# Splitting weight rounding in two steps, moving denominators and T3, and summing attention weights on VectorE and GpSimd instead of by DMA

## The chip, the cores and the metric

The kernel runs on one core of one Trainium2 chip. The metric is the device time of one execution in microseconds, as the median of several runs. Beside it there is a profile of one execution. The engines are called as the profile calls them: PE (TensorE), DVE (VectorE), ACT (ScalarE), POOL (GpSimd) and SP (SyncE, which issues transfers).

## What is computed

The program is an attention block with routing, followed by a bilinear feed-forward block. Each query and each key is assigned to the nearest of 16 centroids, and a query sees only the keys of its own cluster.

```python
batch, n_heads, seq, head_dim = (4, 8, 768, 64)      # 16 clusters
q_assign = np.argmax(np.einsum('bhsd,hcd->bhsc', q_n, c_n), axis=-1)
k_assign = np.argmax(np.einsum('bhsd,hcd->bhsc', k_n, c_n), axis=-1)
mask = q_assign[:, :, :, None] == k_assign[:, :, None, :]
scores = np.where(mask, scale * np.matmul(q, k.transpose(0, 1, 3, 2)), -1e9)
attn = np.exp(scores - np.max(scores, axis=-1, keepdims=True))
attn = attn / (np.sum(attn, axis=-1, keepdims=True) + 1e-09)
x = np.matmul(attn, v)          # heads side by side: 3072 tokens of 512
a = x @ w_a                     # 512 x 1536
b = x @ w_b                     # 512 x 1536
out = (a * b) @ w_out           # 1536 x 512
```

The three weight matrices are float64, and have to be rounded to float32 on the chip.

## The kernel before

Two heads are handled together as a pair. There are 16 pairs, 4 to a batch, and the tokens of a pair are handled in two halves of 384. The main loop goes by groups, six to a pair and so three to a half. In each group TensorE computes two tiles of scores, ScalarE takes their exponential (`pt`, 128 keys by 2 heads by 384 queries), and the tiles of the group before are multiplied with the values. The rest of a group is filled with pieces of the feed-forward block, which belong to the batch before.

```python
for g in range(NG + 3):
    ...
    if 0 < g < NG:
        score(now)                     # TensorE, then the exponential on ScalarE
    check_inverses()
    if 0 < g <= NG:
        for u in before:
            add_up(u)                  # sums of the exponentials over the keys
    if 1 < g <= NG:
        weigh(before)                  # TensorE: times the values
    late = int(g > EARLY)
    if g % 3 == late and 0 < g - late:
        denominators(*divmod(g // 3 - 1, 2))
    ...
    parts = due.get(g, [])             # weight parts to be rounded in this group
    def round_next():
        if parts or not ffn:
            see_w()
        if parts:
            round_w(parts.pop(0))
    round_next()
    ...
    while len(ffn) > least and credit > 0:
        cost, piece = ffn.popleft()
        credit -= cost
        piece()                        # a product of the feed-forward block
        if todo:
            todo.popleft()()           # a step of assignment or normalization
        round_next()
```

The sum over the keys is needed for the denominator. The six tiles (j = 0 to 5) of a half are added into one tile `acc`, whose partitions are then summed by a product with ones. For the pairs of the first batch (p < HP) VectorE adds. For the later ones VectorE adds the first two tiles, and the other four come by accumulating DMAs that GpSimd issues:

```python
def add_up(u):
    p, hf, j = where(u)
    ...
    if j == 1:
        nc.vector.tensor_tensor(out=acc, in0=probs[u - 1], in1=probs[u],
                                op=ALU.add)                        # L595
    else:
        nc.gpsimd.dma_start(out=acc, in_=probs[u], accum_op=ALU.add)  # L598

def denominators(p, hf):
    ps = apart()                       # a bank of the scores' pool
    ... matmul(ones, acc) per head     # L629
    nc.scalar.activation(out=den, in_=ps[:, 0:HB], func=AF.Copy, ...)  # L634
```

The weights are rounded in 36 parts of 128x512. Four instructions on VectorE build the upper part and the remainder, and GpSimd adds both. There is one buffer `rest` and two buffers `raw`. The check of sizes (`see_w`) on ScalarE frees `raw` for the next part.

```python
def round_w(i):
    nc.vector.tensor_scalar(out=wi, in0=hi, ...)                    # L280
    nc.vector.scalar_tensor_tensor(out=wi, in0=hi, in1=wi, ...)     # L283
    rest = wtp.tile([P, WN], FP32, name="rest")
    nc.vector.tensor_scalar(out=rest.bitcast(INT32), in0=wi, ...)   # L287
    nc.vector.scalar_tensor_tensor(out=rest, in0=lo, in1=rest, ...) # L290
    nc.gpsimd.tensor_tensor(out=w, in0=w, in1=rest, op=ALU.add)     # L292
    unseen.append(...)

due = {3 * i + 1: [i] for i in range(8)}
for i in range(8, len(w_parts)):
    due.setdefault(26 + int((i - 8) / 1.5), []).append(i)
```

The feed-forward block multiplies 2 by 2 blocks with seven products instead of eight. For this it needs combinations: T1 to T4 of x (`combine_x`, L779, 128x768, VectorE) and S1 to S4 of the weights (L798, 128x256, VectorE). The products come in the order p1, p2, p6, p5, p7, p3, p4, over three banks. p6 reads T2, p5 T1, p7 T3 and p4 T4. ScalarE copies a first result from its bank (L830), VectorE adds further ones (L834), and GpSimd multiplies a by b (L840). GpSimd also multiplies x by the inverse denominators (L661). In the first batch T2 is made when the last x of the batch is normalized, and T3 with the second product:

```python
        else:                                    # ffn_ready, first batch
            h = h_first
            combine_x(0, "T2")
            ffn.extend(ups_first + plain_ups(0, h, range(NF - 4, NF)))
...
            elif n == 0:                         # ffn_ups, first batch
                ps[1] = both(ps[1], lambda: combine_x(b, "T3"))
                ps[3] = both(lambda: combine_x(b, "T4"), ps[3])
```

A downward stage of each batch (`ffn_downs`) multiplies with w_out in the same manner; its combinations are L929 (weights) and L938 (h).

Of the kernel before, what the change touches and what calls it, by code (L numbers as in the profile page):

```python
# [8 lines left out]
FP32 = mybir.dt.float32  # L9
BF16 = mybir.dt.bfloat16  # L10
INT32 = mybir.dt.int32
UINT32 = mybir.dt.uint32
INT64 = mybir.dt.int64
AF = mybir.ActivationFunctionType
ALU = mybir.AluOpType
# [127 lines left out]
def short_path(nc, tc, ctx, c, cn, centroids_in, casts, n_far, q, k, v,  # L143
# [121 lines left out]
    def load_w(i):  # L265
        if i >= len(w_parts):
            return
        raw = rawp.tile([P, WN], INT64, name="raw")
        nc.sync.dma_start(out=raw, in_=w_parts[i][1])
        raws[i] = raw  # L270

    def round_w(i):
        w = w_parts[i][0]
        wi = w.bitcast(INT32)
        raw = raws.pop(i)
        halves = lambda dt: raw.bitcast(dt).rearrange("p (n two) -> p n two", two=2)
        lo, hi = halves(UINT32)[:, :, 0], halves(INT32)[:, :, 1]


        nc.vector.tensor_scalar(out=wi, in0=hi, scalar1=3, scalar2=0x3FFFFFF8,  # L280
                                op0=ALU.logical_shift_left,
                                op1=ALU.bitwise_and)
        nc.vector.scalar_tensor_tensor(out=wi, in0=hi, scalar=SIGN_TOP, in1=wi,  # L283
                                       op0=ALU.bitwise_and, op1=ALU.bitwise_or)

        rest = wtp.tile([P, WN], FP32, name="rest")
        nc.vector.tensor_scalar(out=rest.bitcast(INT32), in0=wi,  # L287
                                scalar1=SIGN_EXP, scalar2=None,
                                op0=ALU.bitwise_and)
        nc.vector.scalar_tensor_tensor(out=rest, in0=lo, scalar=2.0 ** -52,  # L290
                                       in1=rest, op0=ALU.mult, op1=ALU.mult)
        nc.gpsimd.tensor_tensor(out=w, in0=w, in1=rest, op=ALU.add)  # L292
        unseen.append((i, halves(FP32)[:, :, 1]))

    unseen = []

    def see_w():

        while unseen:
            i, upper = unseen.pop()
            size = spare()[0].bitcast(BF16)[:, 3 * WN:4 * WN]
            nc.scalar.activation(out=size, in_=upper, func=AF.Abs)
            n = 4 * NPAIR + i
            nc.scalar.activation(out=size, in_=size, func=AF.Relu, scale=-STEEP,
                                 bias=edge[:, 0:1], accum_out=stat[:, n:n + 1])
            load_w(i + 2)

    NSTAT = 4 * NPAIR + len(w_parts)  # L310
    edge = zero.tile([P, 1], FP32, name="edge")
# [271 lines left out]
    def add_up(u):  # L583
        p, hf, j = where(u)
        if j == 0 or j == NJ - 1 and p < HP:
            return
        if j == 1:
            accs[p, hf] = accp.tile([P, 2, HB], FP32, name="acc")
        acc = accs[p, hf]
        if p < HP:  # L590
            nc.vector.tensor_tensor(out=acc, in0=probs[u - 1] if j == 1 else acc,  # L591
                                    in1=probs[u], op=ALU.add)
            return
        if j == 1:
            nc.vector.tensor_tensor(out=acc, in0=probs[u - 1], in1=probs[u],  # L595
                                    op=ALU.add)
        else:
            nc.gpsimd.dma_start(out=acc, in_=probs[u], accum_op=ALU.add)  # L598

    def weigh(us):  # L600
        for u in us:
# [141 lines left out]
    def spare():  # L743
        if "spare" not in W:
            W["spare"] = [combp.tile([P, n], FP32, name=name) for name, n in (
                ("pair", 2 * WN), ("comb", 2 * P))]
        return W["spare"]
# [25 lines left out]
    def combine_x(b, name):  # L773
        x = xTs[b]
        l, r = {"T3": (x[:, 2:4, HB:S], x[:, 0:2, HB:S]),
                "T1": (x[:, 0:2, HB:S], x[:, 0:2, 0:HB]),
                "T2": (x[:, 2:4, HB:S], W["T1"]),
                "T4": (x[:, 2:4, 0:HB], W["T2"])}[name]
        nc.vector.tensor_tensor(out=W[name], in0=l, in1=r, op=ALU.subtract)  # L779

    def ffn_ups(b, h):
# [109 lines left out]
        for n, (combinations, ps) in enumerate(parts):  # L891
            if n == 0 and b:
                ps[0] = both(*combinations, ps[0])
                ps[2] = both(lambda: combine_x(b, "T4"), ps[2])
            elif n == 0:
                ps[1] = both(ps[1], lambda: combine_x(b, "T3"))
                ps[3] = both(lambda: combine_x(b, "T4"), ps[3])
            if n + 1 < len(parts):
                for i, step in enumerate(parts[n + 1][0], 4):
                    ps[i] = both(ps[i], step)  # L900
            pieces += [(2 * HB, f) for f in ps]
# [10 lines left out]
    def ffn_downs(b, h):  # L912
# [96 lines left out]

        def before():  # L1010
            see_w()
            assert not raws
            down_room()
            tiles[0][0]()
            combine_w("T1", "12", "11")
            combine_w("T2", "22", "T1")
# [13 lines left out]
    def both(*fs):  # L1030
        return lambda: [f() for f in fs]
# [5 lines left out]
    def early_steps():  # L1037
        combinations = []

        def begin():  # L1040
            early_room(h_first)
            steps, pieces = ffn_ups(0, h_first)
            ups_first.extend(pieces)
            combinations.extend(steps)

        last = HP * GPP
        return {last - 8: lambda: (begin(), combine_x(0, "T1")),
                last: lambda: [f() for f in combinations[0:2]],
                last + 1: lambda: combinations[2]()}

    def ffn_ready(p, hf):

        b, hp = divmod(p, HP)
        if hp < HP - 1 or hf == 0:
            return
        if b > 0:
            h = []

            ffn.insert(len(ffn) - FREE_ROOM, (0, lambda: (
                up_room(b), combine_x(b, "T3"), combine_x(b, "T1"))))  # L1060
            ffn.insert(len(ffn) - 1, (0, lambda: combine_x(b, "T2")))
            ffn.extend(ffn_ups(b, h)[1])
        else:
            h = h_first
            combine_x(0, "T2")
            ffn.extend(ups_first + plain_ups(0, h, range(NF - 4, NF)))
        ffn.extend(ffn_downs(b, lambda: h))

# [14 lines left out]

    due = {3 * i + 1: [i] for i in range(8)}
    for i in range(8, len(w_parts)):
        due.setdefault(26 + int((i - 8) / 1.5), []).append(i)
    early = early_steps()

    for _ in range(12):
        nc.tensor.matmul(out=idle[0:D, 0:D], lhsT=ones, rhs=ones, start=True,  # L1090
# [31 lines left out]
    for g in range(NG + 3):  # L1122
        p, l = divmod(g, GPP)
        if l == 0:
            ready = prep_steps(p + 1)
        now = (2 * g, 2 * g + 1)
        before = (2 * g - 2, 2 * g - 1)
        if g == 1:
            weigh(before)
        if 0 < g < NG:  # L1130
            score(now)
# [3 lines that stand above are left out]
                add_up(u)  # L1135
        if 1 < g <= NG:
            weigh(before)
        late = int(g > EARLY)
        if g % 3 == late and 0 < g - late:
            denominators(*divmod(g // 3 - 1, 2))  # L1140
        if g < NG:
            ready[l]()
        parts = due.get(g, [])
        if g in early:
            todo.append(early[g])

        def round_next():
            if parts or not ffn:
                see_w()
            if parts:  # L1150
                i = parts.pop(0)
                round_w(i)

        round_next()
        if g <= EARLY:
            first, second = 4, 1
        else:
            first, second = 5, 3 if g < NG else 2
        ph = {first: (p, 0), second: (p - 1, 1)}.get(l)
        halved = ph in den_of  # L1160
        if halved:
            todo.extend(normalize(*ph))
        if ffn:
            credit += PER_GROUP[(g > 2 * BG + 3) + (g > 3 * BG + 3)]
            least = FREE_ROOM if halved and ph[1] and (ph[0] + 1) % HP == 0 else 0
# [3 lines that stand above are left out]
                piece()  # L1169
                if todo:  # L1170
                    todo.popleft()()
                round_next()
        else:
            credit = 0
        round_next()
        while todo:
            todo.popleft()()
        if halved:
            ffn_ready(*ph)
        if l == 0 and p + 1 < NPAIR:  # L1180
            if p and not by_blocks(p + 1):
                prep_transpose(p + 1, 2)
            load(p + 2)
        if l == 4 and p + 1 < NPAIR and not by_blocks(p + 1):
            prep_onehot(p + 1, 0)
# [265 lines left out]
```

## Time and profile before

| | |
|---|---|
| time, median of 3 runs | 1055.83 us (1055.52 to 1056.8) |
| span of the profiled execution | 1052.8 us |
| mean granted clock of TensorE | 0.995 |
| exponential, L572 (ScalarE) | 192 x 808 ns |
| accumulating DMA, L598: issue on GpSimd, landing | 96 x 862 ns, 4.0 us |
| first add of a later half, L595 (VectorE) | 24 x 1042 ns |
| multiplication a by b, L840 (GpSimd) | 66 x 1110 ns |
| rounding, L290 (VectorE), L292 (GpSimd) | 36 x 692 ns, 36 x 1402 to 1434 ns |

The profile gives for each engine the time in which it was busy, and for a group of equal instructions their number and mean duration. Idle time before an instruction is put down to what ended it. "A <- B: x, n, y" means that A waited for B for x us in total, n times, at most y us. A row of busy times by stretch has, after the bounds and the length, the busy time of PE, of PE's weight loads, of DVE, ACT and POOL, each with the number of instructions, then the granted clock of TensorE, the busy share of the DMA engines and GB/s. A row of the timeline has the start, the duration, the engine, the line and the operation, and in brackets the idle time before it.

### The profile page before, as it was taken

How to read it: one execution, taken by the hardware profiler on the slowest of the kernel's cores; microseconds unless marked ns; L12 is line 12 of the kernel's file. 1: busy time of each engine (PE TensorE's matmuls, PEld its weight loads, DVE VectorE, ACT ScalarE, POOL GpSimd, SP SyncE). 2: the span in 40 equal slices, each digit the busy share in tenths (PEclk: the TensorE clock that was granted, in tenths of full speed). 3: DMA queues.
4: the chain of work that ended last, by engine and by line, in shares of the span. 5: the costliest groups of instructions: out<-in, count | busy, mean ns of one | idle time of the engine just before them, and what ended most of it. 6: DMA issues, size and time to landing. Idle time of an engine off the chain costs nothing.

```text
span 1052.8 us, 17688 instructions
## 1 busy us (share of the span) xinstructions
PE 1023.8 (97%) x7094; PEld 499.5 (47%) x7094; DVE 579.2 (55%) x1098; ACT 336.5 (32%) x674; POOL 254.1 (24%) x251
## 2 busy tenths in 40 slices
PE   8999989989999999999999999999999999999997
PEld 5443333334445554444444655444444566444564
DVE  6668777786658345443545535444443635444552
ACT  5666544444542213333233121233232201111100
POOL 1112234354332112222324211232222110212100
PEclk9999989999999999999999999999999999999999
DMA  7334546857574463626243372533322320000000
GB/s 181 87 83 88 102 90 147 167 129 154 140 156 86 94 112 65 109 46 106 54 81 65 78 134 54 91 61 66 60 45 50 76 56 21 1 1 1 6 31 29
DMA packets 134346, 84.24 MB, mean 80 GB/s; under 512 B 108144, under 2 KB 117360, under 8 KB 134256
## 3 DMA queue, kind: packets, MB, share of 16 engines
q0 software_dynamic: 13824, 37.75, 19.8%
q1 hardware_dynamic: 120016, 44.85, 19.0%
q8 instruction: 58, 0.95, 0.4%
q10 hardware_dynamic: 416, 0.43, 0.1%
q14 instruction: 32, 0.26, 0.1%
HBM read 37.78 MB, written 6.29 MB: 42 GB/s over the span
## 4 chain that ended last, share of the span: by engine, by line
PE 80%; DMA 6%; DVE 6%; issue 4%; POOL 2%; ACT 2%; DVEq 0%; POOLq 0%; SPq 0%; ACTq 0%
PE m L692 54%; PE s L563 12%; PE O L606 10%; DMA acc<-pt 5%; PE s L629 1%; PE m L629 1%; PE s L378 1%; DVE acc L591 1%; ACT pt L572 1%; PE m L378 1%; POOL xT L661 0%; DVE acc L595 0%; POOL acc L598 0%; POOL h L840 0%; PE m L362 0%
## 5 line engine op out<-in xcount | busy, mean ns | idle before, releaser
L572 ACT ACTIVATE pt<-s 128x768 f32<-128x768 f32 x192 | 146.2, 808 | 191.1 <-PE s L563 142.6
L598 POOL DMA_DIRECT2D acc<-pt x96 | 82.8, 862 | 261.1 <-DMA acc<-pt 161.5
L606 PE MATMUL O<-pt,v 128*64 128x384 f32 x768 | 145.0, 499 | 0.0
L563 PE MATMUL s<-qkT 64*128 64x384 f32 x768 | 140.3, 484 | 0.0
L840 POOL TENSOR_TENSOR h<-h,ha 128x384 f32<-128x384 f32 x66 | 72.8, 1110 | 214.6 <-DVE ha L834 213.7
L834 DVE TENSOR_TENSOR ha<-ha,m 128x384 f32<-128x384 f32 x88 | 48.1, 549 | 126.7 <-PE m L692 100.9
L830 ACT COPY h<-m 128x384 f32<-128x384 f32 x88 | 42.2, 480 | 213.3 <-PE m L692 209.9
L834 DVE TENSOR_TENSOR h<-h,m 128x384 f32<-128x384 f32 x88 | 48.2, 547 | 100.9 <-PE m L692 73.5
L606 PEld LDWEIGHTS O<-pt,v 128*64 128x64 f32 x768 | 46.6, 136 | 85.8 <-issue 77.9
L692 PE MATMUL m<-wo_sb,h 128*64 128x256 f32 x768 | 86.7, 379 | 0.0
L692 PE MATMUL m<-xT,wa_sb 128*64 128x384 f32 x480 | 83.7, 487 | 2.7 <-DVE ha L834 2.5
L563 PEld LDWEIGHTS s<-qkT 64*128 64x128 f32 x768 | 71.0, 188 | 31.8 <-issue 0.9
L692 PE MATMUL m<-xT,wb_sb 128*64 128x384 f32 x480 | 83.1, 486 | 0.4 <-DVE h L834 0.4
L692 PE MATMUL m<-raw 128*64 128x384 f32 x432 | 78.9, 486 | 0.0
L692 PEld LDWEIGHTS m<-wo_sb,h 128*64 128x64 f32 x768 | 56.1, 137 | 29.1 <-issue 3.7
L661 POOL TENSOR_TENSOR xT<-xT,acc 128x384 f32<-128x384 f32 x32 | 35.2, 1099 | 133.4 <-DVE acc L656 84.1
L692 PE MATMUL m<-xT,h 128*64 128x256 f32 x576 | 64.6, 379 | 0.0
L692 PE MATMUL m<-xT,pair 128*64 128x384 f32 x352 | 64.5, 487 | 0.0
L830 ACT COPY ha<-m 128x384 f32<-128x384 f32 x66 | 31.6, 478 | 98.8 <-PE m L692 93.2
L692 PEld LDWEIGHTS m<-xT,wa_sb 128*64 128x64 f32 x480 | 34.9, 137 | 46.1 <-issue 33.2
L692 PEld LDWEIGHTS m<-xT,wb_sb 128*64 128x64 f32 x480 | 34.6, 137 | 43.5 <-issue 37.0
L692 PEld LDWEIGHTS m<-xT,h 128*64 128x64 f32 x576 | 42.1, 137 | 21.4 <-issue 1.6
(180 smaller groups left out, 1323.6 us busy)
## 6 DMA issues: line engine op xcount, KB each, us to landing
acc<-pt POOLq DMA_DIRECT2D x96, 384.0 KB, 4.0
raw<-in_moe_w_a_dram SPq DMA_DIRECT2D x12, 512.0 KB, 4.2
raw<-in_moe_w_b_dram SPq DMA_DIRECT2D x12, 512.0 KB, 3.7
raw<-in_moe_w_out_dram SPq DMA_DIRECT2D x12, 512.0 KB, 3.9
qk<-in_q_dram SPq DMA_DIRECT2D x48, 96.0 KB, 3.3
qk<-in_k_dram SPq DMA_DIRECT2D x48, 96.0 KB, 3.7
v<-in_v_dram SPq DMA_DIRECT2D x24, 192.0 KB, 3.9
out_dram<-rest SPq DMA_DIRECT2D x24, 128.0 KB, 1.7
```

What stands on the lines that cost most here:

```text
L378: nc.tensor.matmul(out=ps[32 * kq:32 * kq + 32, 0:HB], lhsT=cTb[:, hp, :], rhs=qkTs[p][:, kq * HB:(kq + 1) * HB], start=True, stop=True)
L563: nc.tensor.matmul(out=s[:, a, 0:HB], lhsT=Ts[p][r, S + j * P:S + (j + 1) * P], rhs=Ts[p][r, hf * HB:(hf + 1) * HB], start=start, stop=not ...
L572: nc.scalar.activation(out=pt, in_=s[:, :, 0:HB], func=AF.Exp, scale=SCALE)
L591: nc.vector.tensor_tensor(out=acc, in0=probs[u - 1] if j == 1 else acc, in1=probs[u], op=ALU.add)
L598: nc.gpsimd.dma_start(out=acc, in_=probs[u], accum_op=ALU.add)
L606: nc.tensor.matmul(out=O_of[0][a * D:(a + 1) * D, 0:HB], lhsT=vs[p][:, a, j, :], rhs=probs[u][:, a, :], start=(j == 0), stop=(j == NJ - 1))
L629: nc.tensor.matmul(out=ps[a * D:(a + 1) * D, 0:HB], lhsT=ones, rhs=t[:, a, :], start=(n == 0), stop=(n == len(terms) - 1))
L661: nc.gpsimd.tensor_tensor(out=x, in0=x, in1=den, op=ALU.mult)
L692: nc.tensor.matmul(out=ps[half], lhsT=lhsT[:, half], rhs=rhs, **kw)
L830: nc.scalar.copy(out=box[name], in_=box["X"][:, 0:HB])
L834: nc.vector.tensor_tensor(out=box[name], in0=box[name], in1=box[bank][:, 0:HB], op=ALU.add)
L840: nc.gpsimd.tensor_tensor(out=to, in0=to, in1=box[name], op=ALU.mult)
```

## The change

Four things change. A part of the weights is rounded in two steps, `first` and `second`, with products between them, and the steps run after products and no longer ahead of a group's first one; parts fall due at 1.6 instead of 1.5 a group. The denominators are computed behind the second product of a group. T3 is made right behind T2 in the first batch. The sums of the later batches are made by VectorE and GpSimd, by heads: VectorE takes the first head up to j = 3, GpSimd the second head, and both heads for j = 4 and 5. The purpose is that products find their operands and banks ready, and that the sums need no transfers.

```diff
     def round_w(i):
...
+        def first():
+            see_w()
+            hi = halves(INT32)[:, :, 1]
+            nc.vector.tensor_scalar(out=wi, in0=hi, ...)
+            nc.vector.scalar_tensor_tensor(out=wi, in0=hi, ...)
+
+        def second():
+            rest = wtp.tile([P, WN], FP32, name="rest")
+            nc.vector.tensor_scalar(out=rest.bitcast(INT32), in0=wi, ...)
+            nc.vector.scalar_tensor_tensor(out=rest, ...)
+            nc.gpsimd.tensor_tensor(out=w, in0=w, in1=rest, op=ALU.add)
+            unseen.extend(see_steps(i))
+
+        return [first, second]
...
-        if j == 1:
-            nc.vector.tensor_tensor(out=acc, in0=probs[u - 1], in1=probs[u],
-                                    op=ALU.add)
-        else:
-            nc.gpsimd.dma_start(out=acc, in_=probs[u], accum_op=ALU.add)
+        for a in range(2):
+
+            eng = nc.gpsimd if a == 1 or j > 3 else nc.vector
+            eng.tensor_tensor(
+                out=acc[:, a, :],
+                in0=probs[u - 1][:, a, :] if j == 1 else acc[:, a, :],
+                in1=probs[u][:, a, :], op=ALU.add)
...
             elif n == 0:
-                ps[1] = both(ps[1], lambda: combine_x(b, "T3"))
                 ps[3] = both(lambda: combine_x(b, "T4"), ps[3])
...
             combine_x(0, "T2")
+            combine_x(0, "T3")
             ffn.extend(ups_first + plain_ups(0, h, range(NF - 4, NF)))
...
-        due.setdefault(26 + int((i - 8) / 1.5), []).append(i)
+        due.setdefault(26 + int((i - 8) / 1.6), []).append(i)
...
-        if g % 3 == late and 0 < g - late:
-            denominators(*divmod(g // 3 - 1, 2))
+        halves = [divmod(g // 3 - 1, 2)] if g % 3 == late and 0 < g - late else []
+
+        def sums_across():
+            while halves:
+                denominators(*halves.pop())
+
+        if not ffn:
+            sums_across()
+        pieces = 0
...
-        round_next()
+        if not ffn:
+            see_w(1)
+            round_next()
...
                 piece()
                 if todo:
                     todo.popleft()()
-                round_next()
+                for _ in range(cost // HB // 2):
+                    round_next()
+                pieces += 1
+                if pieces == 2:
+                    sums_across()
         else:
             credit = 0
-        round_next()
+            round_next()
+        sums_across()
```

More of the change, by code (lines that the diff above doesn't have):

```diff
@@ L274, in round_w @@
         wi = w.bitcast(INT32)
[L275 to L304, printed above, removed]
+        halves = lambda dt: raws[i].bitcast(dt).rearrange(
+            "p (n two) -> p n two", two=2)
+        def first():
+            see_w()
+            hi = halves(INT32)[:, :, 1]
+            nc.vector.tensor_scalar(out=wi, in0=hi, scalar1=3, scalar2=0x3FFFFFF8,
+                                    op0=ALU.logical_shift_left,
+                                    op1=ALU.bitwise_and)
+            nc.vector.scalar_tensor_tensor(
+                out=wi, in0=hi, scalar=SIGN_TOP, in1=wi, op0=ALU.bitwise_and,
+                op1=ALU.bitwise_or)
@@ new lines, in second @@
+        def second():
+            rest = wtp.tile([P, WN], FP32, name="rest")
+            nc.vector.tensor_scalar(out=rest.bitcast(INT32), in0=wi,
+                                    scalar1=SIGN_EXP, scalar2=None,
+                                    op0=ALU.bitwise_and)
+            nc.vector.scalar_tensor_tensor(
+                out=rest, in0=halves(UINT32)[:, :, 0], scalar=2.0 ** -52, in1=rest,
+                op0=ALU.mult, op1=ALU.mult)
+            nc.gpsimd.tensor_tensor(out=w, in0=w, in1=rest, op=ALU.add)
+            unseen.extend(see_steps(i))
@@ L305, in see_w, with see_steps, first, second @@
+        return [first, second]
+    unseen = deque()
+    def see_steps(i):
+        size = spare()[0].bitcast(BF16)[:, 3 * WN:4 * WN]
+        def first():
+            upper = raws[i].bitcast(FP32).rearrange("p (n two) -> p n two", two=2)
+            nc.scalar.activation(out=size, in_=upper[:, :, 1], func=AF.Abs)
+        def second():
             n = 4 * NPAIR + i
@@ L307, in see_w @@
                                  bias=edge[:, 0:1], accum_out=stat[:, n:n + 1])
+            del raws[i]
             load_w(i + 2)
+        return [first, second]
+    def see_w(steps=None):
+        for _ in range(len(unseen) if steps is None else min(steps, len(unseen))):
+            unseen.popleft()()
     NSTAT = 4 * NPAIR + len(w_parts)
@@ L1011, in before @@
             see_w()
-            assert not raws
+            assert not raws and not rounding
             down_room()
@@ L1085, in short_path @@
     for i in range(8, len(w_parts)):
-        due.setdefault(26 + int((i - 8) / 1.5), []).append(i)
+        due.setdefault(26 + int((i - 8) / 1.6), []).append(i)
     early = early_steps()
+    rounding = deque()
     for _ in range(12):
@@ L1138, in short_path @@
         late = int(g > EARLY)
-        if g % 3 == late and 0 < g - late:
-            denominators(*divmod(g // 3 - 1, 2))
+        halves = [divmod(g // 3 - 1, 2)] if g % 3 == late and 0 < g - late else []
[5 more added lines that the diff above has]
+        pieces = 0
         if g < NG:
             ready[l]()
-        parts = due.get(g, [])
+        for i in due.get(g, []):
+            rounding.extend(round_w(i))
         if g in early:
@@ L1147, in round_next @@
         def round_next():
[L1148 to L1152, printed above, removed]
-        round_next()
+            if rounding:
+                rounding.popleft()()
+        if not ffn:
+            see_w(1)
+            round_next()
         if g <= EARLY:
```

## Prediction

> **What bounds the kernel now.** I read the busy shares first, then the waits of TensorE, then the busy time of each engine by stretch, and last the timeline around the longest wait.
>
> The first part of the page and the head of the chain of waits:
>
> ```profile
> PE 1023.8 (97%) x7094; PEld 499.5 (47%) x7094; DVE 579.2 (55%) x1098; ACT 336.5 (32%) x674; POOL 254.1 (24%) x251
> ...
> PE 80%; DMA 6%; DVE 6%; issue 4%; POOL 2%; ACT 2%; DVEq 0%; POOLq 0%; SPq 0%; ACTq 0%
> ```
>
> TensorE is busy for 1023.8 of 1052.8 us. A busy TensorE need not run at its peak, so I checked the pace: in undisturbed stretches the chain shows 40 matmuls of 384 columns in 6.45 us, 161 ns each, at 143 us as at 808 us. Nothing in the diff changes the number of matmuls, so only the 29 us without a matmul, and stretches at a lower clock, can be won. Some 7 us of them are the tail after the last matmul, 3 us lie in the first 20 us, and 3.7 us between 20 and 125 us, ahead of the feed-forward products. The diff touches little there.
>
> The rest are waits in the feed-forward part. The waits of TensorE (total us, times, longest us):
>
> ```profile
> PE m L692 <- DVE h L779: 5.6, 1, 5.6
> PE s L629 <- DMA acc<-pt: 4.9, 4, 1.8
> PE m L692 <- DVE ha L834: 2.5, 2, 2.3
> ...
> PE m L692 <- ACT ha L830: 1.1, 1, 1.1
> ...
> PE m L692 <- DVE h L834: 0.4, 1, 0.4
> ```
>
> Together 5.6 + 4.9 + 2.5 + 1.1 + 0.4 = 14.5 us. The first is the wait of one product for the combination T3, the second that of the denominators for the accumulating DMAs, the others products that wait for a bank that VectorE or ScalarE has not yet read.
>
> Where do they lie? Busy time by stretch (PE, PEld, DVE, ACT, POOL, then clock, DMA share, GB/s):
>
> ```profile
> 130.00:140.00 10.00, 4.38 (x18) 1.84 (x18) 7.34 (x13) 1.29 (x3) 4.49 (x5) 0.68 0.77 183
> ...
> 125.00:280.00 155.00, 142.15 (x868) 60.02 (x864) 115.90 (x198) 71.23 (x145) 65.30 (x61) 0.98 0.63 140
> ...
> 400.00:570.00 170.00, 170.00 (x1079) 73.94 (x1076) 76.75 (x150) 52.87 (x104) 44.69 (x47) 1.00 0.43 76
> ```
>
> So 155 - 142.15 = 12.9 us of idle TensorE lie in the 155 us in which weights are still rounded beside products. Later TensorE is full: of the waits only two DMA waits, 0.44 us at 367 and 1.52 us at 854, come after 280 us. The row of 130 to 140 us also shows a clock of 0.68. The timeline around it:
>
> ```profile
> 125.68 0.96 DVE L779 TENSOR_TENSOR h<-xT,h 128x768 f32<-128x768 f32 x1 [1.17 <-POOL xT L661]
> ...
> 132.34 0.43 DVE L287 TENSOR_SCALAR rest<-wb_sb 128x512 int32<-128x512 int32 x1 [1.93 <-POOL wa_sb L292]
> ...
> 133.41 0.55 DVE L834 TENSOR_TENSOR h<-h,m 128x384 f32<-128x384 f32 x1
> ...
> 133.87 1.77 DVE L779 TENSOR_TENSOR h<-xT 128x768 f32<-128x768 f32 x1
> ...
> 135.79 2.83 PE L692 MATMUL m<-h,pair 128*64 128x384 f32 x8 [5.62 <-DVE h L779]
> ```
>
> T2 ends at 126.64; T3 starts only at 133.87. Between them VectorE holds two whole roundings (4 instructions of 0.42, 0.69, 0.43 and 0.69 us, 2.2 us each), 1.9 us of waiting for GpSimd to give back the one buffer `rest`, and an add. After the wait eight matmuls take 2.83 us where eight elsewhere in this timeline take 1.46, of which 1.29 until the next eight (8 x 161 ns), and the next twelve score matmuls 2.63 us instead of 1.72. That is a further 1.5 + 0.9 = 2.4 us of slow clock. This one place costs 8.0 us.
>
> **What the Trainium skill says.** "TensorE: Matmul & The Clock Gate", part 1 (the clock gate): an idle window of about 3.4 us halves TensorE's clock until it has been busy for as long. The trace agrees: after 5.62 us idle the clock falls, after the waits of 1 to 2.3 us it stays at 1.00. "SBUF — State Buffer", section "Who interferes with whom": a VectorE instruction with two inputs in SBUF and a GpSimd one that reads SBUF exclude each other for a whole instruction; with one input in PSUM they do not. The trace agrees. Of the 176 combinations of weights (L798, two inputs in SBUF) I paired each with GpSimd's spans: the 53 beside a GpSimd tensor_tensor take 735 ns, the other 123 take 415. The adds from PSUM (L834) take 537 and 551. "GPSIMD Engine Reference", section 3.1 (elementwise): two-input operations are about twice as slow there as on VectorE. The trace: 1110 ns (L840) against 549 ns (L834) on 128x384. "DMA: Bandwidth & Descriptors", rules for kernel authors: an accumulating DMA must have ended before another touches the same bytes. So the four of a half run one after the other: 96 at 4.0 us, and GpSimd idles 161.5 us for them.
>
> **The change, part by part.**
>
> *T3 behind T2.* T3 follows at about 126.6 and takes 0.95 us, or up to 1 us more if a GpSimd operation is in its way. It is there by 127.6 to 128.6. Its product would start at 128.71 + 1.29 = 130.0 us. The wait of 5.6 us and the slow clock of 2.4 us fall away: 8.0 us.
>
> *Sums on VectorE and GpSimd.* There are 12 pairs with 2 halves each, 24 halves. Per half, one VectorE add of 128x768 (1.04 us) and 4 DMAs (862 ns of GpSimd issue each, 3.4 us) leave. In come 10 adds of 128x384: 3 on VectorE (j = 1 to 3, first head, 0.55 us: 1.65 us) and 7 on GpSimd (1.1 us: 7.7 us). VectorE +0.6 us per half, 15 us in all; GpSimd +4.3 us, 102 us in all. A half lasts three groups, 25 to 30 us, so neither fills by the count alone. The last adds (j = 4, 5) are 4 x 1.1 = 4.4 us of GpSimd against two DMAs of 4 us and more, and the denominators come a group and two products later. The 4.9 us of DMA waits go.
>
> *Denominators behind the second product.* No work is added; they start some 2.6 us later, and what they wait for gains as much. They take one of the two score banks for a while, which ScalarE frees before the next score by the spacing of a group (about 10 us).
>
> *Rounding in two steps.* Same instructions. The longest lump of rounding on VectorE between two products is 1.1 us instead of 2.2, and a second step finds `rest` free more often (VectorE waited 3.4 + 5.0 + 2.7 = 11 us for it, by the three L287 rows). The waits for L834 and L830 (2.5 + 0.4 + 1.1 = 4.0 us) should shrink. Rounding is also due at 1.6 parts a group instead of 1.5.
>
> *What it costs.* The shared port. From 125 to 280 us GpSimd's tensor_tensor time is 14.3 (L840) + 29.6 (L292) + 5.0 (L661) + 2.7 (L492) = 51.5 us. Five halves lie there (20 DMA issues), so 5 x 7 x 1.1 = 38.5 us come on top: 90 us, 58% of the stretch instead of 33%. Adding up, for each shape on VectorE, what each took above its undisturbed time gives 17 us in this stretch. In proportion to GpSimd's time this grows by 17 x 38.5 / 51.5 = 13 us. VectorE then has 115.9 + 13 + 5 x 0.7 (sums, at the undisturbed 0.95 us of the old add) + 2 more parts x 2.2 = 137 us. A stretch without waits would be 155 - 12.9 - 2.4 = 140 us long. That is 98%: VectorE all but becomes the bound there, and products will wait for it again. I estimate, by choice and not by a count, that 7 us of such waits remain or arise.
>
> *The sum.* Won between 125 and 280 us: 12.9 + 2.4 - 7 = 8.3 us. Won later: 0.4 + 1.5 = 1.9 us. Lost: about 1.5 us at the first products of each downward stage, where VectorE already shows 10.0 of 10 us busy (320 to 330) and the GpSimd adds come in between. Net 8.7 us; I take 8.3, since the stretch before 125 us may lose a little by its reordered rounding. 1055.8 - 8.3 = 1047.5 us.
>
> **Rivals.**
>
> *VectorE becomes the bound.* The shared port is overbooked between 125 and 280 us and the new waits eat what the old ones gave back. For it: the 98% above, and 2.3 us of wait already at 222 us where a combination took 1.19 us beside L292. Against it: a VectorE operation with one input in PSUM runs beside GpSimd undisturbed, and the rounding ends two groups sooner. Result: 1054 to 1062 us.
>
> *Everything hides.* The spread rounding lets products pass and GpSimd's adds fall beside PSUM reads. Then the 15.3 us of the stretch and the 1.9 us later are won almost whole: 1039 to 1041 us. Against it: the load just counted.
>
> *The DMA sums were never in the way.* They hold TensorE for 4.9 us in all. Then the gain is that of T3 alone, 8 us, less what GpSimd's adds cost: 1048 to 1053 us. This lies close to my own figure, and only the profile tells them apart.
>
> **Range and chances.** TensorE's count of matmuls sets a floor: all waits after 20 us with the slow clock are 14.5 + 2.4 + 3.7 = 20.6 us, under 2% of 1055.8 (21.1 us), so faster by over 2% is nearly excluded. Slower by over 2% would need VectorE to hold TensorE by 30 us more than reckoned. I put the range from 1041.5 (14 us won) to 1055 (nothing left): 0.03 faster, 0.93 within 2%, 0.04 slower.
>
> **What would show it.** Right: no wait for L779 near 130 us and a clock of 1.00 there; no wait for a DMA `acc<-pt`; a row for halves of `acc` on VectorE x72 near 0.55 us and on GpSimd x168 near 1.1 us; VectorE at 9 of 10 in the stretch to 280 us, L798's mean above its 511 ns of now; TensorE idle there some 7 us. Wrong: waits of TensorE for L834, L798 or the new adds that sum to over 12 us; a stretch near 320 or 570 us no longer full; or a new wait of scores for a bank or for a `pt` buffer that GpSimd holds too long.

## The result and the profile after

The changed kernel takes 1047.93 us (median of 4 runs, 1047.16 to 1048.67) against 1055.67 us before. The ratio is 0.9933, 95% interval 0.9907 to 0.9958. That is 0.4 us from the predicted 1047.5 us and inside the range. Run once more beside other kernels, it gave 0.9948 (0.9933 to 0.9962), which is 5.3 us (1047.91 against 1053.17, 11 runs of the kernel before). So the gain is 5 to 8 us where 8.3 was predicted, and the hit to 0.4 us is in part luck. The parts of the sum did not come out as predicted: several were off and cancelled.

In the changed kernel lines have moved: the combinations of x are L801 (before L779), those of the weights L820 (L798), the adds from a bank L856 (L834), the sums L617 (L595 and L598), the denominators L651 (L629) and their copy on ScalarE L656.

The page after, busy time of the engines and the head of the chain of waits:

```profile
PE 1024.5 (98%) x7094; PEld 495.5 (47%) x7094; DVE 652.2 (62%) x1146; ACT 334.2 (32%) x674; POOL 357.0 (34%) x323
...
PE 20%; DVE 0%; issue 0%
```

TensorE has the same 7094 matmuls and the same busy time to 0.7 us, so the 6.2 us that the span lost (1052.8 to 1046.6) are waits and clock, as the prediction held. VectorE has 73 us more and GpSimd 103 us more. The chain of this profile is followed over its last fifth only and says nothing of the middle. What TensorE waited for (total us, times, longest):

```profile
PE m L714 <- DVE ha L856: 6.6, 5, 2.7
PE m L714 <- DVE h L856: 1.9, 2, 1.0
PE s L583 <- ACT acc L656: 1.7, 4, 0.4
PE m L651 <- DVE acc L611: 1.3, 1, 1.3
PE m L714 <- DVE h L801: 1.3, 1, 1.3
```

The wait of 5.6 us for T3 and the 4.9 us for the DMAs are gone. In their place stand 8.5 us of waits for VectorE's adds (2.9 us before) and a new one of 1.7 us: the scores wait four times, all after 300 us, for ScalarE to copy the denominators out of a bank of the scores' pool. By stretch:

```profile
130.00:140.00 10.00, 7.78 (x46) 2.98 (x44) 9.90 (x16) 4.71 (x11) 4.48 (x4) 1.00 0.36 107
...
150.00:160.00 10.00, 7.31 (x36) 2.69 (x34) 9.93 (x16) 3.12 (x6) 7.49 (x7) 0.83 0.32 84
...
125.00:280.00 155.00, 145.12 (x888) 60.95 (x886) 147.34 (x214) 73.50 (x151) 91.40 (x76) 0.99 0.39 95
```

From 125 to 280 us TensorE is idle for 155 - 145.1 = 9.9 us (12.9 before), while VectorE went from 116 to 147 us of 155: it is the second bound of this stretch. The timeline shows why. The start, with T2, T3 and the product that reads T3:

```profile
123.37 2.66 POOL L617 TENSOR_TENSOR acc<-acc,pt 128x384 f32<-128x384 f32 x2
123.44 1.74 DVE L801 TENSOR_TENSOR h<-xT,h 128x768 f32<-128x768 f32 x1 [1.18 <-POOL xT L683]
...
125.10 1.75 DVE L801 TENSOR_TENSOR h<-xT 128x768 f32<-128x768 f32 x1
...
127.93 1.49 PE L714 MATMUL m<-h,pair 128*64 128x384 f32 x8
...
153.97 2.83 PE L714 MATMUL m<-xT,wa_sb 128*64 128x384 f32 x8 [2.69 <-DVE ha L856]
```

T3 is ready in time and its product starts with no wait. But both combinations take 1.75 us instead of 0.95, since GpSimd's two sums lie beside them, and 26 us later TensorE waits 2.69 us for an add and then runs eight matmuls at the slow clock.

A way to see where time is won and lost is the start of the scores of each group, less the same in the kernel before (us, from the two timelines):

| group | 20 | 26 | 27 | 28 | 29 | 34 | 41 | 70 | 95 | end |
|---|---|---|---|---|---|---|---|---|---|---|
| changed | -2.2 | -2.2 | -9.2 | -7.2 | -2.9 | -4.3 | -5.6 | -5.0 | -3.7 | -6.2 |

The feed-forward products begin in group 26, and group 41 begins at 281 us. So 2.2 us were won before any of the waits that I had listed; T3 then brought 7.0 us, of which 6.3 were given back within two groups (5.0 in the second profile of the changed kernel, the last of the experiments, which has no slow clock there).

### The profile page after: what moved, and what is told of

It reads as the page before. It is cut to its first block, busy times and chain, and to the rows that moved or that the text cites. A ratio compares the mean times of both kernels' runs of the same rounds, so it can differ in the third digit from the quotient of the medians.

```text
span 1046.6 us, 17744 instructions
## 1 busy us (share of the span) xinstructions
PE 1024.5 (98%) x7094; PEld 495.5 (47%) x7094; DVE 652.2 (62%) x1146; ACT 334.2 (32%) x674; POOL 357.0 (34%) x323
## 5 line engine op out<-in xcount | busy, mean ns | idle before, releaser
L617 POOL TENSOR_TENSOR acc<-acc,pt 128x384 f32<-128x384 f32 x144 | 159.0, 1124 | 45.5 <-ACT pt L592 42.9
L856 DVE TENSOR_TENSOR ha<-ha,m 128x384 f32<-128x384 f32 x88 | 48.2, 549 | 115.6 <-PE m L714 87.2
L856 DVE TENSOR_TENSOR h<-h,m 128x384 f32<-128x384 f32 x88 | 48.2, 548 | 85.7 <-PE m L714 59.8
```

The lines of the kernel that those rows point to most:

```text
L617: eng.tensor_tensor(out=acc[:, a, :], in0=probs[u - 1][:, a, :] if j == 1 else acc[:, a, :], in1=probs[u][:, a, :], op=ALU.add)
L856: nc.vector.tensor_tensor(out=box[name], in0=box[name], in1=box[bank][:, 0:HB], op=ALU.add)
```

## The experiments

**T3 alone.** The kernel before, with one line moved:

```diff
-                ps[1] = both(ps[1], lambda: combine_x(b, "T3"))
             combine_x(0, "T2")
+            combine_x(0, "T3")
```

> The kernel before with T3 made behind T2 and nothing else. If the one long wait for T3 and the slow clock after it were worth 8 us on their own: 1047 to 1049 us, no wait for L779 near 130 us, and the score matmuls that began at 138.6 us begin near 130.5. Rival (the work that VectorE owed at that point only moves, and later products wait for it instead): the same early start, but half or more of it given back within the next four groups, 1051 us or more in all.

Measured: 1049.49 us, ratio 0.9960 (0.9943 to 0.9978). The lead is 7.3 us at group 27 and 4.4 us from group 28 on. Part of it is given back at once, with the sums still by DMA, so GpSimd's adds are not needed for that. Neither expectation is met in full: some 60% of the local gain stays.

**The sums by DMA again, all else changed.**

```diff
-        for a in range(2):
-            eng = nc.gpsimd if a == 1 or j > 3 else nc.vector
-            eng.tensor_tensor(out=acc[:, a, :], ...)
+        if j == 1:
+            nc.vector.tensor_tensor(out=acc, in0=probs[u - 1], in1=probs[u], ...)
+        else:
+            nc.gpsimd.dma_start(out=acc, in_=probs[u], accum_op=ALU.add)
```

> The changed kernel with the later batches' sums by accumulating DMA again; T3, the late denominators and the two-step rounding stay. Theory of the shared port (GpSimd's adds block VectorE): VectorE's busy time from 125 to 280 us falls from 147 to about 130 us, TensorE's idle time there from 9.9 to 4 us or less, and the time is 1041 to 1045 us, faster than the changed kernel. Rival (the transfers were the cost, and GpSimd's adds are what won): the waits of the denominators for the DMAs come back, some 5 us, and the time is 1050 us or more.

Measured: 1048.87 us, ratio 0.9959 (0.9946 to 0.9972). VectorE stands at 118 us in the stretch, as the theory of the shared port wanted, and the lead of 10 us is kept to group 31 (10.7 us). Yet TensorE is idle there for 11.8 us, not for 4, and the time is no better than the changed kernel's. The rival's waits did not come either (0.7 us for DMAs). By group 34 the whole lead is lost, in a third way. Two of TensorE's waits, one of ScalarE's, and three lines of the timeline:

```profile
PE m L712 <- ACT ha L850: 7.3, 3, 4.8
PE s L649 <- ACT pt L592: 3.6, 1, 3.6
```

```profile
ACT pt L592 <- DMA acc<-pt: 42.2, 15, 6.4
```

```profile
198.64 0.81 ACT L592 ACTIVATE pt<-s 128x768 f32<-128x768 f32 x1 [3.29 <-DMA acc<-pt]
...
203.12 0.81 ACT L592 ACTIVATE pt<-s 128x768 f32<-128x768 f32 x1 [3.66 <-DMA acc<-pt]
...
206.49 2.83 PE L712 MATMUL m<-h,comb 128*64 128x384 f32 x8 [4.78 <-ACT ha L850]
```

The DMAs, one after the other, hold the four `pt` buffers. The next exponential waits for a buffer, and the copy of a product (L850) stands behind it in ScalarE's queue, so TensorE's bank is not freed. With the waits of TensorE at 176 and 202 us its clock is also halved, for 3.4 and 6.8 us. In the kernel before, the same wait of ScalarE was 13.4 us in 7, and it reached TensorE once at most, for 1.1 us: at 177.5 us a product waits for a copy that stands behind a check of sizes and an exponential held for 2.8 us. A fifth buffer would have been the direct test; it was not tried.

**The sums alone.** The kernel before with the sums as changed (the diff above, reversed).

> The kernel before with only the sums moved to VectorE and GpSimd. Theory of the shared port: the 4.9 us of waits for DMAs go, but VectorE in the stretch from 125 to 280 us goes from 116 to 140 us or more and TensorE waits for it; T3's wait stays; 1055 to 1062 us, not faster than before. Rival (transfers were the cost): 1050 to 1052 us.

Measured: 1055.3 us, ratio 1.0016 (1.0007 to 1.0025). VectorE from 125 to 280 us has 136.4 us (115.9 before), less than the 140 us expected. As the theory of the shared port had it, the waits for DMAs go, T3's wait stays and even grows, and the waits for adds grow. The mean clock of its runs is 0.991 (0.994 for the kernel before beside it), so part of what is lost is slow clock. TensorE's waits in that stretch:

```profile
PE m L694 <- DVE h L781: 7.2, 1, 7.2
PE m L694 <- DVE ha L836: 4.5, 2, 2.4
```

By themselves these sums on both engines gain nothing.

**Whole roundings.** The changed kernel, where a part is rounded in one go:

```diff
-        return [first, second]
+        return [lambda: (first(), second())]
```

> The changed kernel with each weight part rounded in one go (four VectorE instructions in a row) wherever its first step stood; all else stays. If the size of the lump matters: TensorE's waits for L856 rise by 2 to 4 us, 1050 to 1052 us. Rival (only the sum of VectorE's work matters, as it is busy 95% there anyway): within 1 us of the changed kernel's 1047.9.

Measured: 1051.87 us, ratio 0.9983 (0.9974 to 0.9992), against 0.9933 and 0.9948 for the changed kernel. Undoing the steps costs 4 to 5 us (0.9983 less either, times 1053), so the time is as expected, but the way is not: the waits for L856 did not rise (6.7 us, against 8.5 in the changed kernel). Instead the lead of 10.0 us at group 27 falls to 4.6 at group 28, behind a wait of 3.5 us for a combination of x, and the clock is halved for 6.8 us from 135.1 us on. On VectorE a whole rounding of 2.2 us, from 131.5 us on, stands ahead of that combination:

```profile
134.33 2.02 DVE L801 TENSOR_TENSOR h<-xT,h 128x768 f32<-128x768 f32 x1
...
136.49 2.83 PE L714 MATMUL m<-h,wa_sb 128*64 128x384 f32 x8 [3.47 <-DVE h L801]
```

With whole roundings a part is also finished one product sooner; the size of the lump and this pace were not separated.

**Denominators first.** The changed kernel with them ahead of the products:

```diff
-        if not ffn:
-            sums_across()
+        sums_across()
         pieces = 0
```

> The changed kernel with the denominators computed ahead of the group's products, as before. With the sums on the engines no DMA is waited for, so the later place should matter little: at most one or two waits of the denominators for GpSimd's last adds or for an exponential, under 1.5 us each, ratio to before 0.993 to 0.996 (the changed kernel: 0.9933). Rival (the later place is what frees the products): waits for acc that sum to 4 us or more, ratio 0.997 or more.

Measured: 1046.16 us, ratio 0.9918 (0.9903 to 0.9934). The waits of the scores for L656 are gone; one of 0.4 us of the denominators for GpSimd's last add comes in. So the late place isn't what wins. It rather costs: four waits of 0.44 us. The ratio is below the expected range, but its interval overlaps that of the changed kernel, so the gain in time is not settled by this run alone.

**VectorE up to j = 3, DMA for the last two.**

```diff
+        if j <= 3:
+            nc.vector.tensor_tensor(out=acc, in0=probs[u - 1] if j == 1 else acc,
+                                    in1=probs[u], op=ALU.add)
+        else:
+            nc.gpsimd.dma_start(out=acc, in_=probs[u], accum_op=ALU.add)
```

> The changed kernel with the later sums on VectorE for both heads up to j = 3 (three adds of 128x768) and by accumulating DMA for j = 4 and 5 only; GpSimd adds nothing. With all four by DMA (the second run) ScalarE waited 42 us for DMAs that still held a pt buffer, and TensorE for the copies behind it. If that is the cause: VectorE's adds free the pt buffers, TensorE's waits for ScalarE near 176, 202 and 237 us go, VectorE in 125 to 280 us stands near 128 us, the lead of 10 us at the 27th group is kept, ratio 0.989 to 0.992, faster than the changed kernel. Rival (any DMA in the chain holds TensorE): waits of 4 us or more for the last two DMAs remain, ratio 0.995 or more.

Measured: 1049.05 us, ratio 0.9949 (0.9934 to 0.9964). VectorE has 129.4 us, as expected, but two DMAs are enough to hold ScalarE for 29.4 us in 8 waits. TensorE's longest waits:

```profile
PE s L649 <- ACT pt L592: 4.1, 1, 4.1
PE s L649 <- DMA acc<-pt: 3.6, 2, 2.9
```

Not the expected gain but the rival is met: here even two DMAs a half hold TensorE once products come faster.

**All sums on VectorE.** Five adds of 128x768 a half; GpSimd adds nothing and issues nothing.

```diff
+        nc.vector.tensor_tensor(out=acc, in0=probs[u - 1] if j == 1 else acc,
+                                in1=probs[u], op=ALU.add)
```

> The changed kernel with all later sums on VectorE alone (five adds of 128x768 a half, 4.75 us). VectorE gets 3.1 us a half more of its own work than in the changed kernel (15 us in the stretch from 125 to 280 us), but GpSimd's adds are gone and with them their blocking. Theory of the shared port: the weight combinations return to near 510 ns from 604, VectorE in that stretch stands at 140 us or less, and the time is no worse than the changed kernel's, ratio 0.990 to 0.994. Rival (only the count of VectorE's work matters, blocking is small): VectorE over 147 us there, ratio 0.996 or more.

Measured: 1045.1 us, ratio 0.9908 (0.9892 to 0.9923). The stretch, and VectorE's sums:

```profile
125.00:280.00 155.00, 146.91 (x904) 62.03 (x900) 145.84 (x228) 74.90 (x154) 54.50 (x43) 0.99 0.38 96
```

```profile
L614 DVE TENSOR_TENSOR acc<-acc,pt 128x768 f32<-128x768 f32 x96 | 106.2, 1106 | 2.4
```

The time is what the theory of the shared port gave, VectorE's load is not: 145.8 us, not 140. What changed is its content. I add up, for each shape, what it took above its undisturbed time (the tenth percentile of that shape): 45.8 us of 147 in the changed kernel, 26.6 of 146 here, 17.4 of 116 before. The weight combinations are back at 494 ns on average. So VectorE does 17.7 us more of its own work within about the same time (119.2 for 101.5 us), because 19.2 us less are lost to blocking.

**The check of sizes in two steps, alone.** The kernel before, with ScalarE's two activations of a check in separate calls ahead of the feed-forward part:

```diff
-            if parts or not ffn:
+            if parts:
                 see_w()
+            elif not ffn:
+                see_w(1)
```

> The kernel before with only the check of sizes on ScalarE (two activations and a read of the accumulator, 1.6 us in a row) cut in two steps before the feed-forward part begins. In the changed kernel the 26th group began 2.2 us earlier, and the waits of the scores for exponentials (2.0 us, 6 times) were gone; so they were in the runs with the two-step code, and not in those without. If the check's length is the cause: those waits go and the 26th group begins 2 us earlier, ratio 0.997 to 0.999. Rival (the place of the rounding on VectorE is the cause): no change before 125 us, ratio 0.999 to 1.001.

Measured: 1051.28 us, ratio 0.9971 (0.9961 to 0.9981). The 26th group begins 2.9 us earlier. Waits of TensorE from 20 to 125 us, first before, then in this run:

```profile
PE s L563 <- ACT pt L572: 2.0, 6, 0.4
PE m L629 <- DVE acc L591: 1.3, 1, 1.3
```

```profile
PE m L634 <- DVE acc L596: 1.3, 1, 1.3
```

A check of 1.6 us in a row delayed an exponential, and that the scores. This small part of the change, which the prediction did not count, is worth 3 us.

**T3 late in the changed kernel.**

```diff
             combine_x(0, "T2")
-            combine_x(0, "T3")
...
             elif n == 0:
+                ps[1] = both(ps[1], lambda: combine_x(b, "T3"))
```

> The changed kernel with T3 made with the second product again. With the rounding in single steps less stands ahead of T3 on VectorE (one step of 1.1 us before the second product), but GpSimd's adds block it. If T3's place is worth in the changed kernel what it is worth alone (ratio 0.996, some 4 us): a wait for L801 of 3 us or more near 130 us, ratio 0.996 to 0.998. Rival (the step-wise rounding alone would have mended most of T3's delay): a wait of 2 us or less there, within 1.5 us of the changed kernel.

Measured: 1047.72 us, ratio 0.9945 (0.9930 to 0.9959); the changed kernel beside it on the same chip 1047.91 us, 0.9948. The rival is met. The wait for T3 is only 2.0 us, with no slow clock, and at group 28 both have the same lead (7.4 and 7.5 us). In the changed kernel T3's place is worth nothing.

**VectorE's sums with the denominators first.** The two edits above together.

> The best guess from the runs: T3 behind T2, the rounding and the check in steps, the later sums on VectorE alone, and the denominators ahead of the products. Against the run with the sums on VectorE alone (ratio 0.9908) the scores' waits for the denominators' bank (1.8 us, 4 times) go: ratio 0.989 to 0.9905, 1043 us or so. If the denominators now wait for VectorE's last add instead (it ends some 2 us after the group begins): up to 1 us at each of the five halves in the rounding stretch, ratio 0.991 to 0.993.

Measured: 1041.83 us, ratio 0.9889 (0.9872 to 0.9906). The scores' waits for the copy of the denominators are gone, and none of the denominators for VectorE's last add came in. Against VectorE's sums with the late denominators (0.9908) this is the second time that the early place comes out ahead, again with intervals that overlap.

**The rounding later and denser**, on top of this:

```diff
-        due.setdefault(26 + int((i - 8) / 1.6), []).append(i)
+        due.setdefault(27 + int((i - 8) / 1.7), []).append(i)
```

> The same with the rounding of the later parts due one group later and more densely (from group 27 at 1.7 a group). In the runs before, TensorE lost 4 us between 133 and 140 us, where VectorE holds T3, the sums and the first roundings at once. If the backlog of VectorE at the start of the products is the cause: those waits fall to 1.5 us or less, ratio 0.986 to 0.989. Rival (the backlog only moves to the next groups, VectorE being full up to 215 us): the same time within 1 us.

Measured: 1040.27 us (1040.14 to 1040.39), ratio 0.9873 (0.9855 to 0.9892), the fastest of all. The waits from 133 to 140 us (4.2 us in the run above) are gone and the lead at group 28 is 10.9 instead of 5.6 us. That is 5.3 us more than in the run above; at group 34 it is 3.6 and at the end 1.7 us more. So both expectations hold in part: most of the backlog moves to later groups, some of it is won. What TensorE waits for now:

```profile
PE m L709 <- DVE h L851: 3.8, 5, 1.5
PE m L709 <- DVE ha L851: 3.0, 3, 1.5
```

**The changed kernel again.**

> The changed kernel once more, beside the others on the same chip, as its first interval was wide: ratio 0.992 to 0.995. Spread between executions of the same kernel should show in the ratio, not in the order of the waits: its waits for L856 near 151 and 211 to 219 us come again.

Measured: 1047.91 us, ratio 0.9948 (0.9933 to 0.9962). All its longer waits recur, their totals within 0.5 us. The stretch after the wait of 2.69 us shows a clock of 1.00, where the first profile had 0.83:

```profile
150.00:160.00 10.00, 7.31 (x48) 2.99 (x46) 9.93 (x15) 3.28 (x6) 7.74 (x7) 1.00 0.39 116
```

## Why the prediction was right, and where it was not

*The frame was right.* TensorE's work is fixed, only waits and clock could be won, and so 2% was out of reach. The best kernel of all the runs, 1.3% faster, agrees.

*T3 behind T2: 8.0 us.* The local step held: its wait and the slow clock went, and the lead grew by 7.0 us in that group. What it missed is that the work on VectorE that stood ahead of T3 still has to be done. Alone, the edit keeps 4.4 us; in the changed kernel, where steps of 1.1 us stand ahead of T3 anyway, it keeps nothing. I had booked the whole and taken the return off elsewhere, as "7 us of such waits remain or arise".

*Sums on both engines.* The count was right. GpSimd takes 1.12 and 1.26 us an add for 1.1. VectorE's means of 0.71 and 0.74 us for 0.55 hold the blocking: the 42 of 72 adds with no GpSimd tensor_tensor beside them take 0.55 us, the other 30 take 0.95. The rows:

```profile
L617 POOL TENSOR_TENSOR acc<-acc,pt 128x384 f32<-128x384 f32 x144 | 159.0, 1124 | 45.5 <-ACT pt L592 42.9
...
L617 DVE TENSOR_TENSOR acc<-acc,pt 128x384 f32<-128x384 f32 x48 | 34.1, 711 | 1.2
...
L617 POOL TENSOR_TENSOR acc<-pt 128x384 f32<-128x384 f32 x24 | 30.2, 1260 | 3.4 <-ACT pt L592 2.5
L617 DVE TENSOR_TENSOR acc<-pt 128x384 f32<-128x384 f32 x24 | 17.7, 738 | 14.2 <-POOL xT L683 14.2
```

The mis-sized term is the blocking: 17 us were to grow in proportion to GpSimd's time by 13 us, to 30 us; they became 45.8 us. So VectorE stood at 147 us in the stretch, not 137. The same sum gives 37.1 us for the run with the sums alone and 22.2 us for the run with all else changed. The sums thus add 20 to 24 us, not 13, and the new places of the rounding 5 to 9, which I had not counted: the two instructions of a first step lie beside a GpSimd tensor_tensor in 22 and 13 of 36 cases, before in 6 and 2. The 7 us of waits, which I had chosen and not counted, came out as 9.9 us of idle TensorE.

*Waits for DMAs: 4.9 us.* They went. But the run with DMA sums has only 0.7 us of them and is no faster than the changed kernel: with DMAs the products run into the buffers that the DMAs hold. That is the better reason for sums on an engine, and the prediction did not see it. The rival "the DMA sums were never in the way" is false once products come faster. For the kernel before it stays open, since the run with the sums alone put blocking in the place of the DMA waits.

*Denominators behind the second product.* I said that ScalarE frees the bank before the next score "by the spacing of a group". That failed four times, 0.44 us each, and is one of the signs of being wrong that the prediction named. With sums on the engines the later place gains nothing.

*Rounding in two steps.* A gain, but not by the way named. The waits for adds and copies, 4.0 us, were to shrink; in the changed kernel those for adds are 8.5 us. What undoing the steps brings in, at a cost of 4 to 5 us of time, is a wait for a combination and slow clock. The steps and T3's new place mend in part the same delay: with the steps, T3's place is worth nothing. The steps without the other changes, and the pace of 1.6 parts a group, were not tried alone.

*The stretch before 125 us.* "May lose a little by its reordered rounding" was wrong in sign. It gained 2.2 us, and the check in two steps alone is worth 3 us.

*The sum.* From the starts of the groups: 2.2 us before group 26 (I had -0.4), 3.4 us from there to group 41 (8.3), 0.6 us after it (0.4). In the second profile of the changed kernel the three are 2.5, 4.1 and 0.7 us. So the total came near because an unseen gain stood in for about half of what was lost, and because the first comparison came out 2.5 us larger than the second; both are luck. The rival in which VectorE becomes the bound held a piece: it did, but not so far as to eat everything.

## What to carry to other kernels

When an edit frees a place where an engine waits, follow what that engine and its neighbours still owe over the next few steps: compare starts of groups, not only the wait that went. An addition on GpSimd is not free help for a VectorE that is three quarters busy; here the same sums on VectorE alone were faster. And read the waits of engines off the path, too: the 13 us for which ScalarE waited for buffers cost TensorE 1.1 us at most until products came sooner.

## What was not expected of the hardware

The blocking grew faster than GpSimd's time. From 125 to 280 us, GpSimd's tensor_tensor time grew from 51 to 92 us (1.8 times) and the excess on VectorE from 17.4 to 45.8 us (2.6 times). Part of this is the new place of the rounding: with the sums alone it is 90 us (1.8 times) and 37.1 us (2.1 times). A scalar_tensor_tensor with two inputs in SBUF (L287 of the changed kernel, the second instruction of a rounding) is among the blocked: the 13 beside a GpSimd tensor_tensor take 1459 ns, the other 23 take 692. The Trainium skill, "SBUF — State Buffer", section "Who interferes with whom", speaks of VectorE instructions with two SBUF inputs in general, and this agrees.

The slow clock does not follow from the length of a wait alone. I had read from the trace before that waits of up to 2.3 us leave the clock at 1.00. The same wait of 2.69 us was followed by a mean clock of 0.83 in one profile of the changed kernel and of 1.00 in another. The clock records of the traces show why. In each of the 14 profiles the changes of the clock, between 1.00 and 0.50, lie whole multiples of 3.413 us after the first one (38, 40 and 306 in the kernel before; 43, 44 and 304 in the changed one). I cut TensorE's time into these steps, leaving out about 20 us at either end. Of the steps at full clock, all 14 in which TensorE was busy for less than 40% were followed by the half clock, 2 of the 7 between 41 and 47%, and none above. In the first profile the wait of 2.69 us lay in one step (150.49 to 153.91 us, 23% busy), and the clock fell. In the second a step ended inside it, at 152.91 us, and the two steps were busy for 45% and 77%. In the run with the sums alone a wait of 2.0 us at 326.5 us was enough (37% busy).

The Trainium skill, "TensorE: Matmul & The Clock Gate", part 1, says of the warm-up that the activity window runs freely, so that the same kernel varies from run to run; the steps here agree, for the slowing too. The idle window of about 3.4 us that it names for the slowing is more than was needed here. So my reading that waits of up to 2.3 us are harmless held only for where the steps lay in that execution. It shows in the times: of 86 executions of the kernel before, the 26 with a mean clock of 0.993 took 1054.8 us on average, the 12 with 0.996 took 1052.2.
